# Gate weights in one transfer, and a new order of the work, in a kernel that fuses sparse attention with a mixture of experts

## The chip, the cores and the metric

The kernel runs on one core of a Trainium2 chip. The metric is the device time of one execution in microseconds (us); lower is better. Five engines work beside each other: TensorE (PE in the profile, PEld for its weight loads), VectorE (DVE), ScalarE (ACT), GpSimd (POOL) and SyncE (SP), whose queue here issues nearly all transfers.

## The reference, cut to what matters

Attention over 8 batches of 8 heads, 576 positions of 64 numbers; four heads look at the last 32 positions, four at every 32nd. Its output, 4608 tokens of 512 numbers, goes through a gate that picks one of 8 experts for each token; an expert keeps its 80 best tokens, and all other rows of the result are zero.

```python
scores = scale * np.matmul(q, k.transpose(0, 1, 3, 2))
scores = np.where(masks[None, :, :, :], scores, -1000000000.0)
attn = np.exp(scores - np.max(scores, axis=-1, keepdims=True))
attn = attn / (np.sum(attn, axis=-1, keepdims=True) + 1e-09)
x = np.matmul(attn, v) ...   # (4608, 512)
logits = x @ w_gate          # (512, 8)
expert_idx = np.argmax(logits, axis=1)
for e in range(E):
    ...                      # keep the `capacity` tokens with the largest gate_w
    h = np.maximum(x[tok_idx] @ w1[e], 0.0)
    out[tok_idx] = gate_w[tok_idx, None] * (h @ w2[e])
```

## The kernel before, in words

The kernel is a list of small operations with names, dependencies and an engine each (class `Plan`). A table of names (`ORDER`, lines 1048 to 1110) gives the order in which they are emitted; each engine, and SP's queue, runs its part of the table strictly in that order. A mark behind a name picks the engine (`/V` DVE, `/A` ACT, `/G` POOL) or the PSUM bank (a digit). A number behind a point is the batch.

*Attention, batch by batch.* SP loads the inputs (`lq`, `lk`, `sq`, `sk`, `lv`, `va`, `vb`, lines 340 to 357). For the local heads PE makes the scores (`sl0`, `sl1`, line 367), DVE the maxima and differences (`mx`, `sb`), ACT the exponentials (`ex`), DVE the sums (`sml`), POOL the division (`nl`, line 400), DVE a transpose (`trl`, line 402), POOL and ACT eight copies into place (`c4l`), PE the product with v (`pvl`, line 420), ACT and DVE the copies out of PSUM (`el`). The strided heads go the same way: `ss` (line 450), `mxs`, `sbs`, `exs` (ACT, line 466), `sms` (DVE, line 469), `ns`, `trs` (line 477), `c4s`, `pvs` (line 492), `es`. `va` and `vb` of a batch refill the buffer that `pvs` of the batch before has read.

*Gate and store.* PE multiplies the output by the gate weights (`gt0`, lines 513 and 516), and DVE turns the logits into gates (`ga`, `gb`, `gc`, `gd`). PE transposes the output back (`rl`, `rs`), ACT or DVE copies it into one of three buffers `xn` (`wl`, `ws`, line 202), and SP stores the buffer to a scratch tensor in HBM (`st0`, `st1`, line 613). Since there are three buffers, the copies of store number i wait until store i-3 has landed; the stores are numbered 2·batch + part, so `wl1.7` and `ws1.7` (number 15) wait for `st0.6` (number 12).

*Gate weights.* `wgt` holds the 512×8 gate weights twice, among zeros (`fwgt` fills them), in two layouts. Four transfers, `wgl0`, `wgl1`, `wgs0`, `wgs1` (lines 278 and 280), bring them from the plain matrix, each in 256 runs of 32 bytes; `gt0.0` waits for all four.

*Routing.* After the last batch, `r1` to `r16` find for every expert its tokens: `r3`, `r7`, `r9` on DVE, `r5` on POOL, `r6` on ACT (line 726), `r9` (lines 750 and 756) waiting for `r6`. Then eight gathers fetch the chosen tokens (`g0` to `g7`, line 810), once all stores have landed.

*Experts.* 64 weight chunks of 512 KiB come in by `w0` to `w63` (line 643); 56 of them are split into two half-width parts by ACT (`wh`, line 672) and DVE (`wo`, line 674). PE multiplies (`u`, line 855; `d`, lines 874 to 882). 18 transfers of 512 KiB, `z0` to `z17` (line 622), write zeros over the output before the results are scattered (`s`, line 901). The table puts `w` and `z` wherever SP is to issue them, so both also serve as fillers between the loads of attention.

Of the kernel before, what the change touches and what calls it, by code (L numbers as in the profile page):

```python
# [1048 lines left out]
lq.0 pid lqb.0 pib fkm0/V fkm1/G fwgt/A fkl1/A fkl0/V pm0 lk0.0 lk1.0 fkn0/A fpts1/V lkb1.0 lk0.1 pmc fks0/A lkb0.0  # L1049
lk1.1 pmn/V ps0 fkn1/A tk warm/4 sl0.0 lq.1 wgs0 fks1/G sk1.0 tk1/0 sq.0 mx0.0 sl1.0 sk0.0 sb0.0 lv.0 psc ex0.0 tk2  # L1050
rc1 mx1.0 lk1.2 sl0.1 lk0.2 sb1.0 lq.2 rc2 ex1.0 sl1.1 fpts0/A sml.0 fpsn/A lk0.3 sal.0/V srl.0 ss0.0 mx1.1 sk0.1
nl0.0 fptb0/A sk1.1 mx0.1 ss1.0 wgs1 nl1.0 fptb2/V ss2.0 sq.1 fptb1/G trl.0 ss3.0 sb0.1 c4l4.0/G c4l6.0/A sk1.2 sb1.1
c4l5.0/A lq.3 c4l1.0/G sl0.2 ex0.1 lk1.3 c4l3.0/G mxs.0 ex1.1 sk0.2 c4l7.0/G sbs.0 sl1.2 fzt/A c4l2.0/G sml.1 c4l0.0/G
exs.0 sal.1/V fvs1/A srl.1 sms.0 pvl0.0/1 nl0.1 fvs0/A sas.0/V srs.0 pvl1.0/2 mx0.2 ns1.0 nl1.1 el0.0/A vb.0 mx1.2
pvl2.0/0 va.0 ns0.0 ss0.1 trl.1 lv.1 lq.4 ss1.1 w0 sb0.2 c4l4.1/G c4l7.1/A ss2.1 cap trs.0 c4l1.1/A c4l5.1/G w1 ex0.2
sl0.3 c4l2.1/G wgl1 sb1.2 c4s3.0/G wgl0 ad1.0 ss3.1 c4s0.0/G w2 ex1.2 el1.0/V sq.2 c4s2.0/G ad2.0 c4s1.0/A sml.2
c4l6.1/G c4l3.1/A pvs0.0/1 c4l0.1/G el2.0/A sq.3 sal.2/V srl.2 mxs.1 pvl0.1/2 es0.0/A nl0.2 sk1.3 sbs.1 pvs2.0/0 lk0.4
nl1.2 el0.1/V exs.1 pvl1.1/1 es2.0/V wh0 pvs1.0/2 ad1.1 trl.2 pvl2.1/0 el1.1/A es1.0/A rl0.0/1 lv.2 ad2.1 c4l4.2/G
c4l0.2/A mx0.3 gt0.0/2 lk1.4 c4l5.2/A c4l3.2/G sb0.3 va.1 c4l6.2/A ss0.2 c4l7.2/G vb.1 sms.1 wl0.0/A sl1.3 sk0.3
sas.1/V el2.1/A srs.1 w3 wo0 ex0.3 w4 c4l2.2/A w5 rl0.1/1 xqs.0/V ns0.1 mx1.3 rs0.0/0 wl0.1/A ss1.2 sb1.3 ns1.1  # L1060
c4l1.2/A xql.0/G ss2.2 trs.1 ex1.3 pvl0.2/1 ws0.0/A sml.3 c4s2.1/G lt.0 st0.0 rl1.0/0 c4s0.1/G ss3.2 sal.3/V el0.2/A
c4s3.1/G srl.3 wl1.0/V pvl1.2/2 c4s1.1/A xql.1/G nl0.3 mxs.2 pvs0.1/1 ad1.2 pvl2.2/0 el1.2/A nl1.3 es0.1/V pvs1.1/2
ad2.2 sbs.2 pvs2.1/1 el2.2/A es1.1/A trl.3 rs1.0/0 vb.2 exs.2 sl0.4 lq.5 es2.1/A sms.2 w6 c4l1.3/G wh1 sas.2/V
c4l7.3/G srs.2 ws1.0/V wh2 c4l2.3/G sl1.4 mx0.4 c4l4.3/G c4l6.3/A sb0.4 c4l0.3/G gt0.1/2 ns1.2 ex0.4 lk1.6 mx1.4 ns0.2
c4l3.3/A lv.3 rl1.1/1 sb1.4 lk1.5 xql.2/G ss0.3 wo1 va.2 ex1.4 lk0.5 ss1.3 sk0.4 sml.4 rc3 gt1.0/0 z0 ss2.3 lt.1 z1
sal.4/V c4l5.3/A srl.4 z2 trs.2 ss3.3 nl1.4 sk1.4 pvl0.3/2 sq.4 ga.0 c4s0.2/G wl1.1/V pvl1.3/0 el0.3/A c4s1.2/G
c4s2.2/A rs0.1/1 xqs.1/G ad1.3 c4s3.2/G mxs.3 pvl2.3/2 ws0.1/A nl0.4 sbs.3 el1.3/A pvs1.2/1 ad2.3 pvs0.2/0 trl.4
es1.2/A exs.3 pvs2.2/1 el2.3/A c4l7.4/G sms.3 sl0.5 vb.3 es2.2/A c4l2.4/G sas.3/V es0.2/A st0.1 srs.3 c4l1.4/A lv.4
xqs.2/G sl1.5 mx0.5 ns0.3 wh3 st1.0 sb0.5 lq.6 c4l6.4/G lk0.6 rc4 ns1.3 va.3 gt0.2/2 trs.3 sk0.5 ss0.4 x0 mx1.5
c4s2.3/G rs1.2/1 sb1.5 rs1.1/0 ws1.2/A ss1.4 wo2 ex1.5 rs0.2/1 ex0.5 ss2.4 wo3 ws1.1/A ws0.2/A sml.5 c4s0.3/G gt1.1/0  # L1070
rl1.2/1 c4s1.3/G lt.2 ss3.4 c4l5.4/G sal.5/V wl1.2/A srl.5 rl0.2/2 c4l3.4/A c4l4.4/G mxs.4 sk0.6 sl0.6 c4s3.3/A nl0.5
z3 sbs.4 w7 ga.1 exs.4 sk1.5 c4l0.4/G pvs2.3/1 mx0.6 st1.1 wl0.2/A nl1.5 pvl0.4/0 sms.4 sq.5 es2.3/A pvs1.3/2 lk0.7
xql.3/A sas.4/V el0.4/V wh4 st0.2 pvl1.4/1 srs.4 es1.3/V pvs0.3/0 ns0.4 wh5 ad1.4 trl.5 pvl2.4/2 ns1.4 es0.3/A va.4
sl1.6 vb.4 trs.4 c4l7.5/G c4l3.5/A lv.5 c4l1.5/A sq.6 sb0.6 el1.4/A c4s1.4/G gt0.3/0 lk1.7 xqs.3/V c4l4.5/G ex0.6
sk1.6 ad2.4 mx1.6 gt1.2/1 c4l2.5/G lq.7 ss0.5 el2.4/V c4l0.5/G lt.3 sb1.6 rl0.3/2 c4s2.4/G rl2.3/0 ga.2 c4s0.4/G
wl0.3/A rl1.3/1 c4s3.4/G wl2.3/V xql.4/A rs2.3/2 ex1.6 c4l6.5/G ss1.5 ws2.3/V wl1.3/A pvs2.4/0 c4l5.5/A sml.6 pvs1.4/1
es2.4/A pvl0.5/2 wo4 es1.4/A pvs0.4/0 el0.5/A wo5 pvl1.5/1 wh6 vb.5 va.5 pvl2.5/2 sal.6/V srl.6 es0.4/V nl0.6 ss2.5
lv.6 xqs.4/V ad1.5 gb.2 el1.5/A ss3.5 nl1.6 rs0.3/0 ad2.5 sk0.7 mxs.5 el2.5/A sk1.7 gt0.4/1 sbs.5 ws0.3/A st1.2 trl.6
z4 exs.5 sl0.7 z5 z6 sms.5 c4l4.6/G c4l0.6/A gt1.3/2 st0.3 c4l5.6/A sas.5/V c4l2.6/G sl1.7 srs.5 sq.7 mx0.7 c4l6.6/G
z7 sb0.7 z8 c4l1.6/G ga.3 ss0.6 c4l7.6/G ex0.7 mx1.7 lt.4 ns0.5 ss1.6 c4l3.6/A sb1.7 ns1.5 ss2.6 ex1.7 trs.5 ss3.6  # L1080
sml.7 rl0.4/0 c4s3.5/A c4s1.5/G rl1.4/2 ge.2 c4s2.5/G wl0.4/A pvl0.6/1 sal.7/V c4s0.5/G srl.7 wl1.4/A mxs.6 rs1.3/0
nl0.7 el0.6/A sbs.6 gt1.4/2 ws1.3/A nl1.7 pvs2.5/1 ga.4 gc.2 pvs1.5/0 es2.5/A pvs0.5/2 exs.6 pvl1.6/1 es1.5/A sms.6
vb.6 es0.5/A st2.2 pvl2.6/0 sas.6/V srs.6 ad1.6 ns1.6 trl.7 gt0.5/2 el1.6/A ns0.6 lv.7 va.6 ss0.7 trs.6 c4l5.7/A st2.1
lt.5 st1.3 rs1.4/1 c4l7.7/A st2.3 gt1.5/2 c4s0.6/G c4s3.6/A w8 ss1.7 c4l3.7/G ga.5 c4l6.7/A w9 gd.2 ss2.7 c4l2.7/G
ws1.4/A gb.5 c4s2.6/G ss3.7 c4l0.7/G ad2.6 ge.5 el2.6/V rs0.4/2 c4l4.7/A c4s1.6/G mxs.7 rl0.5/1 ws0.4/A gr.2/0 sbs.7
st0.4 pvs1.6/2 gg.2 wl0.5/A st1.4 wo6 pvs2.6/0 exs.7 pvs0.6/1 es1.6/A xql.5/G sms.7 c4l1.7/G es2.6/A rs0.5/2 sas.7/V
va.7 es0.6/A srs.7 rl1.5/0 gc.5 ns1.7 vb.7 ws0.5/A ns0.7 gt0.6/1 st0.5 wl1.5/A trs.7 pvl0.7/2 lt.6 rs1.5/0 el0.7/A
c4s3.7/G pvl1.7/1 c4s1.7/A ws1.5/V c4s2.7/G c4s0.7/A gt1.6/2 st1.5 ad1.7 xqs.6/G el1.7/V pvl2.7/0 wh7 xql.6/G w10
# [62 lines left out]
```

## Time and profile before

| | |
|---|---|
| median of 3 runs | 263.83 us (262.11 to 265.59) |
| the profiled execution | 264.44 us |
| its span in the trace | 262.7 us |
| busy PE, DVE, ACT, POOL | 80%, 77%, 60%, 41% of the span |
| moved by DMA | 84.05 MB |

All times in the trace count from the start of the span; 1.7 us of the execution lie around it. In the timeline a row gives start, duration, engine, line, operation, out<-in, and in brackets the idle time of that engine just before and what ended it. An engine takes its instructions in order, so an idle time in brackets also delays everything behind it on that engine. A row of the stretches gives, for each, its length, the busy time of PE, PEld, DVE, ACT and POOL, the granted TensorE clock (1.00 is full), the busy share of the 16 DMA engines (1.03 is what they reach here) and GB/s.

### The profile page before, as it was taken

How to read it: one execution, taken by the hardware profiler on the slowest of the kernel's cores; microseconds unless marked ns; L12 is line 12 of the kernel's file. 1: busy time of each engine (PE TensorE's matmuls, PEld its weight loads, DVE VectorE, ACT ScalarE, POOL GpSimd, SP SyncE). 2: the span in 40 equal slices, each digit the busy share in tenths (PEclk: the TensorE clock that was granted, in tenths of full speed). 3: DMA queues.
4: the chain of work that ended last, by engine and by line, in shares of the span. 5: the costliest groups of instructions: out<-in, count | busy, mean ns of one | idle time of the engine just before them, and what ended most of it. 6: DMA issues, size and time to landing. Idle time of an engine off the chain costs nothing. (4 is left out here: it accounts for less than half of the span.)

```text
span 262.7 us, 9497 instructions
## 1 busy us (share of the span) xinstructions
PE 209.6 (80%) x4036; PEld 162.8 (62%) x4036; DVE 202.9 (77%) x358; ACT 157.8 (60%) x244; POOL 107.9 (41%) x156
## 2 busy tenths in 40 slices
...
GB/s 160 255 401 392 253 309 405 375 258 287 387 373 231 262 407 328 293 401 237 228 370 216 333 371 298 347 360 419 412 413 408 387 410 384 409 410 408 115 41 43
DMA packets 24783, 84.05 MB, mean 320 GB/s; under 512 B 4321, under 2 KB 4321, under 8 KB 24162
## 3 DMA queue, kind: packets, MB, share of 16 engines
...
q0 software_dynamic: 1024, 2.62, 2.8%
...
## 5 line engine op out<-in xcount | busy, mean ns | idle before, releaser
L204 POOL COPY ptb<-ptl 32x576 f32<-32x576 f32 (+1 forms) x39 | 26.4, 676 | 14.2 <-DVE ptl L402 9.2
L202 ACT COPY xn<-bk 128x512 f32<-128x512 f32 x28 | 16.1, 583 | 19.5 <-DMA xs<-xn 9.9
L420 PE MATMUL bk<-ptb,vl 128*64 128x160 f32 (+1 forms) x288 | 24.5, 307 | 3.3 <-POOL pl L400 1.7
L492 PE MATMUL bk<-pts,vs 128*64 128x72 f32 x512 | 22.5, 248 | 5.3 <-POOL pts L204 1.9
L492 PEld LDWEIGHTS bk<-pts,vs 128*64 128x64 f32 x512 | 21.3, 156 | 7.4 <-issue 3.3
L400 POOL TENSOR_TENSOR pl<-pl,sm 128x576 f32<-128x576 f32 x16 | 18.2, 1150 | 18.6 <-DVE sm L398 13.0
L420 PEld LDWEIGHTS bk<-ptb,vl 128*64 128x64 f32 x288 | 19.1, 140 | 4.9 <-issue 1.9
L450 PE MATMUL sstr<-ks,qs 128*18 128x36 f32 x1024 | 14.8, 199 | 8.2 <-issue 7.7
L202 ACT COPY ptb<-ptl 32x576 f32<-32x576 f32 (+1 forms) x25 | 16.6, 665 | 7.9 <-DVE ptl L402 7.6
L204 POOL COPY pts<-pts 32x576 f32<-32x576 f32 x24 | 17.0, 707 | 9.7 <-DVE pts L477 8.9
L901 POOL DMA_INDIRECT out<-xtl,pl x4 | 4.5, 1123 | 40.0 <-ACT xtl L896 22.3
L450 PEld LDWEIGHTS sstr<-ks,qs 128*18 128x18 f32 x1024 | 11.3, 99 | 12.7 <-issue 10.6
L474 POOL TENSOR_TENSOR psn<-ps,sm 128x64 f32<-128x64 f32 (+1 forms) x16 | 11.5, 738 | 16.7 <-DVE sm L472 6.5
L901 POOL DMA_INDIRECT out<-xts,pl x4 | 4.9, 1234 | 28.9 <-ACT xts L896 23.5
L386 ACT ACTIVATE pl<-pl 128x512 f32<-128x512 f32 (+1 forms) x16 | 10.7, 683 | 9.8 <-DVE pl L383 9.8
L674 DVE SCALAR_TENSOR_TENSOR slot<-slot,slot 128x1024 f16<-128x1024 f32 x13 | 16.0, 1254 | 0.7 <-ACT slot L672 0.6
L855 PEld LDWEIGHTS <-slot 128*128 128x128 f16 x288 | 14.4, 113 | 3.1 <-issue 3.1
L672 ACT ACTIVATE slot<-slot 128x1024 f16<-128x1024 f32 x13 | 13.5, 1054 | 1.1 <-DMA slot<-w 1.0
L202 ACT COPY xts<-bk 128x360 f32<-128x360 f32 (+1 forms) x19 | 9.4, 509 | 7.4 <-PE bk L492 5.6
L202 ACT COPY xtl<-bk 128x416 f32<-128x416 f32 (+2 forms) x17 | 8.2, 479 | 9.5 <-DVE xtl L434 4.3
L195 PE MATMUL sla<-identb 128*128 128x512 bf16 x33 | 10.7, 463 | 2.7 <-DVE identb L256 2.7
L592 PE MATMUL bk<-ident,xtl 128*128 128x128 f32 x64 | 12.4, 325 | 0.4 <-ACT xn L202 0.3
...
## 6 DMA issues: line engine op xcount, KB each, us to landing
...
```

Source lines behind the costliest of these rows:

```text
L195: nc.tensor.matmul(sla.rearrange("p (a b) -> p a b", b=P), identb, identb.unsqueeze(1).broadcast_to([P, 4, P]), start=True, stop=True)
L202: nc.scalar.copy(o, i)
L204: eng[e].tensor_copy(o, i)
L400: op("nl%d.%d" % (u, b), {"POOL": 1.17}, lambda e, u=u: nc.gpsimd.tensor_tensor(pl[:, u], pl[:, u], sm[:, 9 * u:9 * u + 9].unsqueeze(2).br ...
L420: nc.tensor.matmul(t[64 * u:64 * u + 64, n0:n0 + z], tvl[:, u, c], ptb[:, c, u, 0:z], start=(c == 3 * k), stop=(c == 3 * k + 2), tile_posi ...
L450: nc.tensor.matmul(so[32 * g:32 * g + 18, r8], tqs[h][:, g, rr], tks[h][:, :, g, rr], start=False, stop=r8 == 7, tile_position=(0, 32 * g))
L474: op("ns%d.%d" % (i, b), {"POOL": d}, lambda e, js=js, z0=z0, z1=z1, st_=st_: nc.gpsimd.tensor_tensor(psn[:, :, z0:z1:st_], ps[:, :, js], ...
L492: nc.tensor.matmul(t[64 * x:64 * x + 64, c:c + 72], tvs[:, r], pts4[:, 2 * (r % 16) + r // 16].rearrange("p h j -> p (h j)"), start=True, ...
L592: nc.tensor.transpose(t[:, x, c], xv[:, c, x, 128 * a:128 * a + 128] if a < 2 else xql[:, c, x].rearrange("p s b -> p (s b)"), ident)
L672: op("wh%d" % i, {"ACT": 1.05}, lambda e: nc.scalar.activation(hi(i), raw(i), AF.Copy, scale=SC), [st["w%d" % i]] + prev, filler=True)
L674: op("wo%d" % i, {"DVE": 1.24}, lambda e: nc.vector.scalar_tensor_tensor(lo(i), raw(i), SC, hi(i), op0=ALU.mult, op1=ALU.subtract), [st["w ...
L855: nc.tensor.matmul(o[:, f], w[:, n:n + P], x[:, a, c], start=(c == 0 and i == 0 and f == 0), stop=(c == 3 and i == 2), skip_group_check=True)
```

## The change

First, the host packs the gate weights into one array of 128 × 48 numbers, and one transfer `wg` brings it into `lt`, a buffer that is free until `lt.0`. Four small copies, together `wgc`, put the numbers into their places in `wgt`; the table gives them to POOL. `gt0.0` waits for `wgc` instead of four transfers.

Second, the whole table is replaced. Nearly every name stands in another place, and some copies and fills change engine.

```diff
-    for x in range(2):
-        dma("wgl%d" % x, 8192, lambda x=x: nc.sync.dma_start(
-            wgl[:, x::2, E * x:E * x + E], wg[0:256].rearrange("(c p) e -> p c e", p=P)), fills["wgt"])
-        dma("wgs%d" % x, 8192, lambda x=x: nc.sync.dma_start(
-            wgs[64 * x:64 * x + 64, :, E * x:E * x + E], wg[256:512].rearrange("(h d) e -> d h e", d=D)), fills["wgt"])
+    wgp = lt[:, 0:48].rearrange("p (c e) -> p c e", e=E)
+    dma("wg", 24576, lambda: nc.sync.dma_start(lt[:, 0:48], wg), [])
+
+    def wgc(e):
+        for x in range(2):
+            copy(e, wgl[:, x::2, E * x:E * x + E], wgp[:, 0:2])
+            copy(e, wgs[64 * x:64 * x + 64, :, E * x:E * x + E], wgp[64 * x:64 * x + 64, 2:6])
+
+    op("wgc", {"DVE": 0.45, "POOL": 0.8, "ACT": 1.0}, wgc, fills["wgt"] + [st["wg"]])
...
-           ([st[n] for n in ("wgl0", "wgl1", "wgs0", "wgs1")] if b == 0 else []), pairs=16, mode="m32", acquire=True)
+           ([st["wgc"]] if b == 0 else []), pairs=16, mode="m32", acquire=True)
...
-r6 z10 w17 w18 warm/9 r8 w19 r9 w20 z11 wo8 warm/2 r10 z12 z13 r11 wh10 r12 r13 g0 z14 r14 g1 warm/1 r15 z15 r16 wo9
+rs2.7/2 wl2.7/A r5 wl1.7/A rs1.7/0 ws2.7/A ws1.7/A st2.4 st1.7 x0 r6 st2.6 st2.7 st2.5 warm/9 r8 w17 wh7 r9 w18 w19
...
+    wgp = np.concatenate([w_gate[0:256].reshape(2, P, E).transpose(1, 0, 2),
+                          np.tile(w_gate[256:512].reshape(4, D, E).transpose(1, 0, 2), (2, 1, 1))], axis=1).reshape(P, 6 * E)
```

Two places of the new order matter below. The first is ACT around `exs.7`, the exponentials of the last batch. Before, the piece is (L466 is `exs.7`; the copies into `xn` are `wl` and `ws`, here of batches 4 and 5):

```order
L563 ACTIVATE gsm_126<-gsm_126 96x144
L202 COPY ptb_98<-ptl_102 32x18x32
L202 COPY xn_112<-bk_149 128x2x256
L202 COPY xn_111<-bk_148 128x2x256
L466 ACTIVATE ps_105<-ps_105 128x576
L202 COPY xts_108<-bk_149 128x72x5
```

Now it is (L470 is `exs.7`):

```order
L567 ACTIVATE gsm_126<-gsm_126 96x144
L202 COPY ptb_98<-ptl_102 32x18x32
L202 COPY xqs_115<-xts_109 128x128
L470 ACTIVATE ps_105<-ps_105 128x576
L202 COPY xts_108<-bk_149 128x72x6
L202 COPY xts_108<-bk_147 128x72x5
L202 COPY xts_108<-bk_148 128x72x5
L202 COPY xn_111<-bk_149 128x2x256
L202 COPY xn_111<-bk_147 128x2x256
```

The copy into `xn_111`, which waits for a store to land, stood just ahead of the exponentials and now stands four rows behind them.

The second place is SP's queue around `st0.6` (of the rows `xs<-xn` the one from `xn_110` in the last rows of each piece). Before, the transfers ahead of it are (`w` and `zt` are fillers of 512 KiB each):

```order
L643 DMA kl_91<-w 128x1024
L613 DMA xs<-xr_113 32x1024
L643 DMA kl_91<-w 128x1024
L643 DMA ql_89<-w 128x1024
L643 DMA ks_95<-w 128x1024 x2
L622 DMA out<-zt_117 128x1024
L643 DMA qs_93<-w 128x1024
L643 DMA kl_92<-w 128x1024
L613 DMA xs<-xn_110 128x1024
L613 DMA xs<-xn_111 128x1024
```

Now they are:

```order
L617 DMA xs<-xn_111 128x1024
L617 DMA xs<-xn_110 128x1024
L617 DMA xs<-xr_113 32x1024
L626 DMA out<-zt_117 128x1024 x3
L617 DMA xs<-xn_112 128x1024
L626 DMA out<-zt_117 128x1024 x3
L617 DMA xs<-xr_113 32x1024
L617 DMA xs<-xn_110 128x1024
L647 DMA kl_92<-w 128x1024
L617 DMA xs<-xn_112 128x1024
L617 DMA xs<-xn_111 128x1024
```

Eight fillers stood between the large stores and `st0.6`; now three stand directly ahead of it, behind one large store and three more fillers.

## Rows read from the trace of the kernel before

**Rows 1.** The page: its first line, and busy time of the engines

```profile
span 262.7 us, 9497 instructions
...
PE 209.6 (80%) x4036; PEld 162.8 (62%) x4036; DVE 202.9 (77%) x358; ACT 157.8 (60%) x244; POOL 107.9 (41%) x156
```

**Rows 2.** The waits of ACT: for whom, us in total, times, the longest

```profile
ACT xn L202 <- DMA xs<-xn: 9.9, 3, 4.1
...
ACT slot L672 <- DMA kl<-w: 7.9, 2, 5.9
```

**Rows 3.** Timeline of ACT, from 116 to 168 us

```profile
119.61 0.58 ACT L202 COPY xn<-bk 128x512 f32<-128x512 f32 x1 [2.39 <-DMA xs<-xn]
...
135.73 0.58 ACT L202 COPY xn<-bk 128x512 f32<-128x512 f32 x1 [3.41 <-DMA xs<-xn]
136.34 0.68 ACT L466 ACTIVATE ps<-ps 128x576 f32<-128x576 f32 x1
...
161.50 1.56 ACT L202 COPY xn<-bk 128x512 f32<-128x512 f32 x3 [4.09 <-DMA xs<-xn]
162.93 2.13 ACT L726 ACTIVATE pl<-pl,esel 128x80 bf16<-128x80 bf16 x8
```

**Rows 4.** Timeline of DVE, PE and POOL, 121 to 223 us

```profile
121.24 0.35 DVE L532 TENSOR_REDUCE lgs<-bk 96x48 f32<-96x192 f32 x1 [2.38 <-PE bk L527]
...
132.83 0.69 PE L492 MATMUL bk<-pts,vs 128*64 128x72 f32 x15 [0.77 <-DMA vs<-va]
...
137.06 0.75 DVE L469 TENSOR_REDUCE sm<-ps 128x32 f32<-128x576 f32 x1 [2.61 <-ACT ps L466]
...
165.10 0.55 DVE L750 SCALAR_TENSOR_TENSOR pl<-jc,pl 128x320 bf16<-128x320 f32 x1 [3.34 <-ACT pl L726]
...
168.34 1.21 POOL L810 DMA_INDIRECT xtl<-xs,pl  x1 [9.09 <-DVE pl L774]
...
222.52 1.22 DVE L674 SCALAR_TENSOR_TENSOR kl<-kl,slot 128x1024 f16<-128x1024 f32 x1 [5.05 <-ACT slot L672]
```

**Rows 5.** Timeline of SP's queue: stores, fillers and loads with their times of issue

```profile
108.36 3.14 SPq L622 DMA_DIRECT2D out<-zt  x3
111.59 1.19 SPq L613 DMA_DIRECT2D xs<-xn  x1
...
127.82 0.53 SPq L613 DMA_DIRECT2D xs<-xn  x1
...
144.28 0.42 SPq L643 DMA_DIRECT2D kl<-w  x1
...
149.53 0.43 SPq L643 DMA_DIRECT2D kl<-w  x1
153.48 0.83 SPq L613 DMA_DIRECT2D xs<-xn  x2
```

**Rows 6.** Six stretches: length, busy PE PEld DVE ACT POOL, clock, DMA share, GB/s

```profile
34.00:36.00 2.00, 1.58 (x30) 1.38 (x32) 1.90 (x5) 1.28 (x3) 1.86 (x3) 0.76 0.76 296
36.00:38.00 2.00, 1.81 (x20) 1.48 (x18) 1.01 (x2) 0.68 (x1) 1.67 (x2) 0.50 0.69 247
...
122.00:126.00 4.00, 4.00 (x78) 3.90 (x74) 2.69 (x9) 2.43 (x5) 0.81 (x2) 0.78 0.08 26
162.00:164.00 2.00, 0.43 (x2) 0.00 (x0) 0.00 (x0) 2.00 (x8) 0.00 (x0) 1.00 0.16 64
190.00:200.00 10.00, 10.00 (x235) 9.99 (x233) 8.94 (x11) 6.82 (x10) 1.36 (x1) 1.00 1.03 411
...
245.00:262.70 17.70, 11.36 (x228) 10.94 (x225) 10.63 (x13) 6.85 (x10) 3.70 (x3) 0.93 0.12 37
```

**Rows 7.** The gate weights' transfers (ns min/median/max to issue), and a small POOL copy

```profile
L280 SPq DMA_DIRECT2D wgt<-wg x2: 642/652/661, 7.4 to 18.4; - x2
L278 SPq DMA_DIRECT2D wgt<-wg x2: 472/723/974, 31.1 to 32.1; - x2
...
156.56 0.19 POOL L716 CAST pl<-pl 128x16 f32<-128x16 uint32 x1
```

More of the change, by code (lines that the diff above doesn't have):

```diff
@@ L1048 @@
 ORDER = """
[L1049 to L1088, printed above, removed]
```

81 lines of the change are left out of this document (60 added, 21 removed).

## The prediction

> **What bounds the kernel now.** I read the page first, then the waits of ACT, then the timelines of ACT, DVE and SP at the moments those waits name, and last the stretches by DMA share. On the page no engine is full: PE is busy 80% and DVE 77% of 262.7 us [rows 1]. The stretches say why. In 190 to 200 us the DMA engines run at share 1.03 and 411 GB/s [rows 6], and the weight stream looks like that until 245 us; before it, during attention, the same engines have holes (share 0.08 in 122 to 126 us, 0.16 in 162 to 164 us [rows 6]). So the end of the run is set by how many bytes are left when attention is over and by when that is. After the stream 17.7 us remain in which DMA does almost nothing (share 0.12) and PE and DVE finish [rows 6]; that tail stays.
>
> What makes attention late is one kind of wait that stands out among ACT's: copies into `xn` that wait for an older store to land, 9.9 us in three pieces [rows 2]. They end at 119.61, 135.73 and 161.50 us [rows 3]. Their stores (`st0.3`, `st1.3`, `st0.6`) were issued at 111.59, 127.82 and 153.48 us [rows 5]: 8.0, 7.9 and 8.0 us earlier. A store thus takes 8 us to land in this part of the run, and a copy that comes sooner stops ACT, with all that is queued behind it. DVE pays: 2.38 us of idle time before L532 at 121.24, 2.61 us before L469 at 137.06 (it waits for the exponentials `exs.7`, which ran at 136.34, right behind the stopped copy [rows 3]), and 3.34 us before L750 at 165.10 (it waits for `r6`, which ran at 162.93, behind the three copies) [rows 3, 4].
>
> **The change part by part.** The sum is made against the profiled execution's own 264.44 us; that is 0.61 us above the median of the runs, 263.83 us, and the forecast is brought to the median at the end.
>
> *The distance from a store to the copy that needs its buffer.* I count in the table how many DVE entries stand between a store and the first copy that must wait for it. Before: 11, 8 and 4 for the three pairs above. Now: 22, 24 and 5. All other pairs had 6 or more before and showed no wait. The first two waits should therefore go.
> - First wait (`st0.3`): DVE's 2.38 us. It is bounded by 0 (something else is late) and 3.2 us (with the wait that follows it a little later). Next late is POOL, which has the division and the copies of two batches queued there; I take 2.4.
> - Second wait (`st1.3`): the exponentials now stand ahead of the copies, so DVE's 2.61 us go. Next late is the v load of the last batch, whose product PE needs just after; PE already waited once for a load `va`, 0.77 us at 132.83 [rows 4]. Bounds 0 and 2.61; I take the middle, 1.3.
> - Third wait (`st0.6`): the distance is still 5 entries, so the copy comes as early as before. But ahead of the store there were eight fillers, issued from 144.28 to 149.53 us and a little after [rows 5]; one is 524,288 bytes, at 411 GB/s [rows 6] 1.28 us, so 10 us of traffic. Now three fillers stand directly ahead (3.8 us) and three more behind one store further up. Bounds 0 and 3.34; I take half, 1.7.
>
> *A pair that gets closer.* `st0.1` and the copy `wl1.2`: 5 DVE entries now, 7 to the nearest copy before. With 6 and 7 no wait showed, with 8 one of 3.41 us on ACT did [rows 3], because the queue was fuller there. Behind that copy on ACT stand two of the copies that PE's `pvl` of batch 4 waits for. Bounds 0 and 3.41; I take 1.0 lost.
>
> *Fillers.* Of the 82 fillers, 27 are issued before the last `st1.7` in the old table, 29 in the new one. Two fewer remain for the saturated stream: 2 × 1.28 = 2.6 us. The stream can use it, since DVE stood idle for 5.05 us at 217 to 222 us for a weight chunk [rows 4], and ACT 5.9 us for the same [rows 2]. Against it, one split fewer is done ahead of the expert phase (12 instead of 13): 1.22 us more on DVE later [rows 4]. Net 1.4 gained, bounds 0 and 2.6.
>
> *Gate weights.* Four transfers of 256 runs of 32 bytes become one of 128 runs of 192 bytes, and SP issues one row instead of four (0.65 to 0.72 us each [rows 7]). In 34 to 38 us, when two of the four and the `cap` load of 8-byte runs were in the queue, the DMA share was 0.76 and 0.69 [rows 6], a loss of (1.03-0.76)×2 + (1.03-0.69)×2 = 1.2 us for these together; the other two would cost as much at most, so at most 2.4 us. The new transfer has an eighth of the runs. Added are four POOL copies; the nearest small copy takes 0.19 us [rows 7], so 0.8 us on POOL, an engine at 41%, and ahead of the copies for `c4l.2`; uncovered they cost 0.8 us. Bounds: 2.4 gained, 0.8 lost. The early DMA time is worth little, since the same engines have holes later: I take 0.5 gained. Here a page speaks against the change: the Trainium skill, "DMA: Bandwidth & Descriptors", section "Specifications", says that below 512 bytes a run is not moved at line rate but by read-modify-write. By that mark alone 192 bytes are no better than 32, and this term would be nothing; the rows show a loss with short runs but not at which length it ends.
>
> *The sum.* -2.4 -1.3 -1.7 +1.0 -1.4 -0.5 = -6.3 us; 264.44 - 6.3 = 258.1, and 0.6 less on the median's scale: 257.5 us. All other moves I cost at nothing: up to `r1` the entries of both tables hold the same work, within 2 us on each engine (ACT has 4 us less), so what they do is only in which waits they make.
>
> **The rivals.**
>
> *More is gained.* If the new order also closes the holes of the DMA engines, 0.95 × 4 = 3.8 us in 122 to 126 us and 0.87 × 2 = 1.7 us in 162 to 164 us [rows 6] come on top, some 252 us. For it: weight fillers now stand ahead of the `va` and `vb` loads of the last two batches, where SP has to wait for PE and before had little in flight. Against it: the second hole is partly the third wait again.
>
> *No change.* The two waits go, but PE and DVE at 80% and 77% [rows 1] only find the next dependency late, as they do at a dozen smaller places; about a sixth of the sum is left, 263 us. For it: each idle time I count is the last of several things that come within 1 or 2 us. Against it: the two moved pairs do not get a little but twice to three times further apart.
>
> *Slower.* Three fillers now stand ahead of `va.6` and three more ahead of `lv.7` in the one queue. Each three cost 3.8 us of the load behind them. If neither is covered, 7.7 us of attention are lost, the three waits' gain does not show because the loads are later than they were, and only the fillers' 1.4 comes back: 264.44 + 7.7 - 1.4 - 0.6 = 270 us. It decides from the point where `va.6` lands after the last of the copies `c4s.6`. For it: PE has already waited for `va` there [rows 4]. Against it: SP waits for PE before it may issue these loads, and by then the fillers have had time to drain.
>
> **How the numbers follow.** Forecast, 257.5 us, with a range of its own of 254 to 261: 0.50. More gained, about 252: 0.20. No change, about 263: 0.16. Slower, about 270: 0.14. About 2% of the time, 5.3 us, is what a measurement of this kernel can tell from no change: faster means below 258.6, slower above 269.1. Of the forecast's case 0.28 lie below 258.6 and 0.22 above; the first rival adds 0.20 to faster, the second 0.16 to same, the third 0.13 to slower and 0.01 to same. So faster 0.48, same 0.39, slower 0.13. The range reaches into both rivals' sides: 251 to 267.
>
> **What would show each step right or wrong.** In the profile after, ACT's wait for `xs<-xn` should fall from 9.9 us to under 5, and what is left should stand before `r6`; L469 should not wait 2.6 us for the exponentials of the last batch; L750 should begin less than 3 us after the last instruction of `r7`; the first gather, now at 168.34 us [rows 4], should come near 163; the saturated stream should end near 239 us instead of 245. I am wrong if the gather comes no earlier, if the stream ends no earlier although it does, or if a new wait for `vs<-va` or `vl<-vl` of some microseconds stands before L492 or L420.

## The result, and the profile after

The changed kernel takes 251.22 us (median of 4 runs, 248.06 to 253.73), against 263.83 us before: a ratio of 0.9445, 95% interval 0.9316 to 0.9574. Run once more later, it took 250.65 us (248.03 to 253.98, 6 runs; ratio 0.9497, 0.9443 to 0.9552). Medians are of all runs; ratios are of those within 1.5% of the kernel's fastest. The forecast was 257.5 us: the direction is right, the size half of what came by the medians (6.3 of 12.6 us) and less than half by the ratio (14.6 us). The time lies below the forecast's own range, 254 to 261 us, and just inside the wide one, 251 to 267. The profiled execution took 248.06 us, with a span of 246.3 us.

The page after, its first line and the busy time of the engines, to be held against [rows 1]:

```profile
span 246.3 us, 9517 instructions
...
PE 202.8 (82%) x4037; PEld 157.7 (64%) x4037; DVE 206.9 (84%) x359; ACT 156.4 (63%) x243; POOL 108.9 (44%) x160
```

Each engine is busy for as long as before, within 7 us of 210; the span is 16.4 us shorter. So it is mostly idle time that went. The waits of ACT after (for whom, us in total, times, the longest):

```profile
ACT ptb L202 <- DVE ptl L406: 10.7, 3, 4.9
...
ACT slot L676 <- DMA kl<-w: 5.8, 1, 5.8
```

The 9.9 us of copies that waited for stores [rows 2] are gone altogether; the list has no such entry. The wait for a weight chunk in the expert phase is as long as before. The timeline of ACT, DVE, POOL and PE after, at the places that answer to [rows 3, 4]:

```profile
128.23 0.71 ACT L470 ACTIVATE ps<-ps 128x576 f32<-128x576 f32 x1
...
151.95 2.13 ACT L730 ACTIVATE pl<-pl,esel 128x80 bf16<-128x80 bf16 x8 [0.41 <-POOL pl L726]
...
128.97 0.76 DVE L473 TENSOR_REDUCE sm<-ps 128x32 f32<-128x576 f32 x1 [0.97 <-ACT ps L470]
...
154.37 0.54 DVE L754 SCALAR_TENSOR_TENSOR pl<-jc,pl 128x320 bf16<-128x320 f32 x1
...
157.40 1.22 POOL L814 DMA_INDIRECT xtl<-xs,pl  x1 [5.48 <-DVE pl L777]
...
89.75 0.46 PE L454 MATMUL sstr<-ks,qs 128*18 128x36 f32 x32
```

The exponentials of the last batch start 8 us earlier, `r6` 11 us earlier, the mask of `r9` (L754) without a wait, and the first gather at 157.40 instead of 168.34 us. The last row, the first strided scores of batch 5, has no counterpart in the rows of the prediction. Here it is in the kernel before, with SP's queue ahead of it (the first row, `x0`, stores a row of zeros in the scratch tensor):

```profile
77.14 0.48 SPq L283 DMA_DIRECT2D xs<-zt  x1
84.67 0.47 SPq L352 DMA_DIRECT2D ks<-ks  x1
...
88.05 0.43 SPq L350 DMA_DIRECT2D qs<-qs  x1
...
96.26 0.71 PE L450 MATMUL sstr<-ks,qs 128*18 128x36 f32 x32 [1.31 <-issue]
```

SP waited 7.0 us, from 77.6 to 84.67, for PE to finish with the buffer that the load `sk0.6` refills. Behind it stood `sq.5`, a load whose own buffer was free: it went out at 88.05, and the strided scores of batch 5 began at 96.26 us, 6.5 us later than now. That they waited for this load is not named there: the bracket says only "issue". In the changed kernel `sq.5` is issued at 69.64 us:

```profile
69.64 0.45 SPq L354 DMA_DIRECT2D qs<-qs  x1
...
109.80 1.41 SPq L359 DMA_DIRECT2D vl<-vl  x1
111.25 0.43 SPq L647 DMA_DIRECT2D slot<-w  x1
111.73 1.12 SPq L647 DMA_DIRECT2D kl<-w  x2
112.94 0.57 SPq L617 DMA_DIRECT2D xs<-xn  x1
115.39 0.53 SPq L360 DMA_DIRECT2D vs<-va  x1
```

The lower rows are a second place: three weight fillers go out just before SP comes to `va.6`, which has to wait for PE. Before, SP issued nothing from 116.5 to 124.6 us while it waited for PE, and the DMA engines' share fell to 0.08 from 122 to 126 us [rows 6].

What this does to the DMA engines stands in the stretches (columns as in [rows 6]; the share is the last but one). The kernel before:

```profile
0.00:80.00 80.00, 61.99 (x1490) 45.91 (x1491) 67.97 (x117) 48.56 (x75) 50.89 (x80) 0.96 0.90 323
...
80.00:100.00 20.00, 15.81 (x330) 12.61 (x329) 13.46 (x25) 12.18 (x22) 11.26 (x16) 0.91 0.83 299
100.00:120.00 20.00, 15.59 (x417) 12.24 (x417) 17.29 (x29) 10.55 (x19) 11.03 (x14) 1.00 0.92 345
120.00:140.00 20.00, 17.24 (x329) 14.25 (x333) 13.68 (x31) 11.95 (x23) 7.64 (x13) 0.77 0.73 258
140.00:150.00 10.00, 10.00 (x148) 7.06 (x149) 7.41 (x23) 6.08 (x12) 3.74 (x7) 0.96 0.79 274
150.00:160.00 10.00, 7.71 (x50) 5.50 (x51) 8.74 (x39) 5.24 (x9) 3.22 (x12) 1.00 1.02 386
160.00:170.00 10.00, 3.86 (x26) 1.91 (x25) 6.11 (x26) 4.62 (x12) 1.36 (x2) 0.74 0.85 303
```

The changed kernel, with the two holes of [rows 6] and the tail:

```profile
0.00:80.00 80.00, 64.42 (x1534) 47.92 (x1535) 68.96 (x113) 45.14 (x69) 51.47 (x86) 0.96 0.93 337
...
80.00:100.00 20.00, 17.71 (x433) 14.74 (x434) 18.63 (x34) 18.08 (x32) 10.39 (x11) 1.00 0.97 368
100.00:120.00 20.00, 16.91 (x418) 12.24 (x413) 17.71 (x35) 11.52 (x23) 14.34 (x21) 1.00 0.87 313
120.00:140.00 20.00, 16.05 (x298) 13.51 (x300) 14.84 (x38) 10.25 (x21) 10.04 (x16) 0.91 0.95 359
140.00:150.00 10.00, 7.74 (x77) 5.72 (x71) 9.43 (x32) 5.17 (x12) 1.72 (x7) 1.00 1.01 391
150.00:160.00 10.00, 6.49 (x40) 3.18 (x41) 9.47 (x37) 7.46 (x16) 3.76 (x8) 0.88 0.81 289
160.00:170.00 10.00, 7.08 (x66) 4.50 (x64) 6.54 (x10) 5.56 (x8) 4.83 (x4) 0.84 0.99 358
...
122.00:126.00 4.00, 4.00 (x96) 3.37 (x93) 2.87 (x4) 0.19 (x1) 0.21 (x1) 0.68 1.00 384
162.00:164.00 2.00, 0.94 (x5) 0.20 (x3) 0.66 (x1) 0.61 (x1) 1.70 (x2) 1.00 0.91 324
...
233.00:246.30 13.30, 6.67 (x120) 6.15 (x117) 6.98 (x9) 3.52 (x6) 2.75 (x2) 0.87 0.15 45
```

Take 1.03 minus the share, times the length, as idle time of the DMA engines. From 80 to 170 us it was 20 × (0.20 + 0.11 + 0.30) + 10 × (0.24 + 0.01 + 0.18) = 16.5 us and is 8.8; from 0 to 80 us it was 10.4 and is 8.0. The two falls, 7.7 and 2.4, are 10.1 of the 12 us by which the weight stream ends earlier (233 instead of 245 us). The tail behind the stream fell from 17.7 to 13.3 us, 4.4. The holes at 122 to 126 and 162 to 164 us are filled.

The clock column has changed too: from 120 to 140 us TensorE was granted 0.77 before and 0.91 after (a mix of its two levels, 0.50 for 1.2 and 1.00 for 2.4 GHz), over the whole profiled run 0.917 and 0.958. No run holds the clock fixed, so what part of the gain goes with it stays open. It is not what the largest single edit below gave (the fillers moved up as one train): that profile shows 0.907, and the time fell by 7.2 us.

### The profile page after: what moved, and what is told of

It is laid out like the page before. It is cut to its first block, busy times and chain, and to the rows that moved or that the text cites. A ratio compares the mean times of both kernels' runs of the same rounds, so it can differ in the third digit from the quotient of the medians.

```text
span 246.3 us, 9517 instructions
## 1 busy us (share of the span) xinstructions
PE 202.8 (82%) x4037; PEld 157.7 (64%) x4037; DVE 206.9 (84%) x359; ACT 156.4 (63%) x243; POOL 108.9 (44%) x160
## 5 line engine op out<-in xcount | busy, mean ns | idle before, releaser
L204 POOL COPY ptb<-ptl 32x576 f32<-32x576 f32 (+1 forms) x41 | 27.7, 676 | 11.8 <-PE bk L424 5.1
L202 ACT COPY ptb<-ptl 32x576 f32<-32x576 f32 (+1 forms) x23 | 15.3, 666 | 17.2 <-DVE ptl L406 10.7
L496 PE MATMUL bk<-pts,vs 128*64 128x72 f32 x512 | 20.1, 234 | 3.0 <-issue 1.2
L496 PEld LDWEIGHTS bk<-pts,vs 128*64 128x64 f32 x512 | 18.7, 143 | 4.5 <-issue 2.6
L204 POOL COPY pts<-pts 32x576 f32<-32x576 f32 x19 | 15.5, 818 | 10.3 <-DVE pts L481 7.8
L202 ACT COPY xn<-bk 128x512 f32<-128x512 f32 x25 | 13.9, 586 | 4.6 <-PE bk L596 3.3
L678 DVE SCALAR_TENSOR_TENSOR slot<-slot,slot 128x1024 f16<-128x1024 f32 x13 | 16.4, 1289 | 0.3 <-ACT slot L676 0.2
L859 PEld LDWEIGHTS <-slot 128*128 128x128 f16 x288 | 12.7, 104 | 2.6 <-issue 2.6
L478 POOL TENSOR_TENSOR psn<-ps,sm 128x64 f32<-128x64 f32 (+1 forms) x16 | 10.7, 687 | 7.1 <-ACT ptb L202 3.4
L371 PE MATMUL slb<-kl,ql 128*32 128x128 f32 x320 | 12.4, 301 | 1.5 <-issue 1.5
L195 PE MATMUL sla<-identb 128*128 128x512 bf16 x34 | 10.7, 457 | 2.7 <-DVE identb L256 2.7
L406 DVE STREAM_TRANSPOSE ptl<-pl 128x1152 f32<-128x1152 f32 x8 | 10.9, 1367 | 1.9 <-POOL pl L404 1.9
L371 PEld LDWEIGHTS slb<-kl,ql 128*32 128x32 f32 x320 | 9.5, 121 | 4.7 <-issue 4.4
```

Source lines behind the costliest of these rows:

```text
L195: nc.tensor.matmul(sla.rearrange("p (a b) -> p a b", b=P), identb, identb.unsqueeze(1).broadcast_to([P, 4, P]), start=True, stop=True)
L202: nc.scalar.copy(o, i)
L204: eng[e].tensor_copy(o, i)
L371: nc.tensor.matmul(o[32 * g:32 * g + 32, 128 * c - z:128 * c - z + 128], tql[h][:, hh, 32 * t:32 * t + 32], tkl[h][:, :, hh, 32 * t:32 * t ...
L406: op("trl.%d" % b, {"DVE": 1.37}, lambda e: nc.vector.transpose(ptl.rearrange("p u c s q -> p (u c s q)"), pl.rearrange("p u c k -> p (u c ...
L496: nc.tensor.matmul(t[64 * x:64 * x + 64, c:c + 72], tvs[:, r], pts4[:, 2 * (r % 16) + r // 16].rearrange("p h j -> p (h j)"), start=True, ...
```

## The experiments

18 kernels ran. The diffs show the table, mostly SP's part of it alone. Each ratio is to the kernel before, run on the same chip.

**The gate weights.** The changed kernel with the four old transfers:

```diff
-wg
+wgl0 wgl1 wgs0 wgs1
...
-wgc/G
```

> The changed kernel with the four old gate transfers in the place of the one, and without the four POOL copies; nothing else differs. Gate theory: the one transfer was worth what I gave it, 0.5 us, at most 2.4, so 251.7 to 253.6 us, and ACT and PE are late around gt0.0 at 40 us. All other theories: the DMA holes later swallow it, 250.5 to 252 us, no different from the changed kernel.

Measured: 250.65 us, ratio 0.9534 (0.9459 to 0.9609). That is the changed kernel's time; the gate edit is worth nothing that can be told. Its stretches behind the four loads, which SP issues from 30.9 to 33.6 us:

```profile
32.00:34.00 2.00, 1.51 (x58) 1.39 (x44) 1.88 (x5) 1.97 (x4) 1.62 (x3) 1.00 0.84 237
34.00:36.00 2.00, 1.88 (x41) 1.10 (x36) 1.97 (x3) 1.95 (x3) 0.31 (x1) 1.00 1.13 328
36.00:38.00 2.00, 0.01 (x2) 0.01 (x2) 2.00 (x4) 1.47 (x4) 1.51 (x1) 1.00 1.02 334
```

Here all four loads of short runs leave the share at 0.84 to 1.13; in the changed kernel, without them, it is 0.90, 0.99 and 1.00 in the same stretches. The 0.76 and 0.69 of [rows 6], which I had put down to them, were not their doing, or not theirs alone; the `cap` load, which stood beside them there, is at 79 us here.

**Queue or engines?** The two orders taken apart: first the changed kernel's engines with SP's queue of before, then the reverse.

```diff
-sk0.5 lk1.7 z3 lk0.7 st1.1 st0.2 sk0.6 va.4
+sk0.5 x0 sk0.6 z3 w7 sk1.5 st1.1 sq.5 lk0.7 st0.2 va.4
...
```

> The changed kernel's order on PE, DVE, ACT and POOL, but SP's queue in the order of the kernel before (the one gate transfer in the place of the four). Queue theory (the gain is that no load stands behind a blocked entry of SP's queue): about 260 us or more. Engine theory (the gain is in the order of the engines): about 253 us. Store theory (my prediction: stores too close to the copies that need their buffers): the engine distances stay long, the eight fillers ahead of st0.6 and the two fillers fewer come back, +1.7 and +1.4, about 254 us.

> The reverse: the order of the kernel before on the four engines (with the four gate copies put in on POOL), and SP's queue in the order of the changed kernel. Queue theory: 252 to 256 us. Engine theory: 262 us. Store theory: the copies into xn stand as close behind their stores as before, only the fillers ahead of st0.3 and st0.6 differ, about 260 us, with ACT's wait for stores at 5 us or more.

Measured: 283.39 us (1.071, 1.0604 to 1.0817) and 270.64 us (1.0258, 1.0172 to 1.0344). Both mixtures are slower than either kernel. That is "260 us or more" for the queue theory in the first; every other number missed. The DMA engines stood idle for about 44 and 36 us up to 170 us, against 27 in the kernel before (1.03 minus the share of that stretch, as above). A queue served strictly in order and the engines it waits for are one order; a half of each tells nothing of what the other half is worth. So I went on with small edits of the kernel before.

**The store waits, my theory.** All three waits taken away by the distances that I had counted, on the kernel before:

```diff
-st1.2 z4 z5 z6 st0.3 sq.7 z7 z8 vb.6 st2.2 lv.7 va.6 st2.1 st1.3 st2.3
+st1.2 st0.3 z4 z5 z6 sq.7 z7 z8 st1.3 vb.6 st2.2 lv.7 va.6 st2.1 st2.3
...
-wl0.5/A exs.7 es1.6/A es2.6/A
+exs.7 es1.6/A es2.6/A wl0.5/A
...
-w10 st2.0 w11 w12 w13 w14 z9 w15 w16 st0.6 st1.6
+w10 st2.0 st0.6 st1.6 w11 w12 w13 w14 z9 w15 w16
```

> The kernel before with only its three store waits taken away: three fillers put behind st0.3, wl0.5 behind es2.6, st1.3 ahead of vb.6, seven fillers put behind st1.6. Store theory: ACT's wait for stores falls from 9.9 us to under 3 and the time by 2.4 + 1.3 + 1.7 = 5.4 us, to 258.4 us. Queue theory and engine theory: the waits go but little else, 261 to 264 us.

Measured: 263.47 us, ratio 0.9965 (0.9916 to 1.0014): no change. The waits did go (0.3 us are left), the last strided transpose (`trs.7`, L477) ran 4.4 us earlier (136.04 instead of 140.39 us), and then this stood in POOL's timeline, with these stretches before it:

```profile
170.47 1.21 POOL L810 DMA_INDIRECT xtl<-xs,pl  x1 [15.50 <-DMA out<-zt]
...
120.00:140.00 20.00, 16.54 (x357) 12.81 (x358) 16.28 (x35) 13.37 (x25) 10.59 (x18) 1.00 0.89 328
140.00:150.00 10.00, 8.70 (x125) 6.76 (x124) 8.41 (x35) 5.92 (x13) 1.35 (x2) 1.00 0.36 120
```

The seven fillers that I put behind `st1.6` left a new hole at 140 to 150 us (share 0.36), and then stood ahead of the last six stores. `r11` had the gathers' row numbers ready at 159.8 us (159.62 + 0.16); the last 10.7 us of the gather's 15.5 are its wait for those stores. The profile names a filler (`out<-zt`) instead, but the gather depends on none. The wait had moved, and the idle time of the DMA engines with it: their share from 0 to 170 us is 0.87, as in the kernel before.

The same without the third piece, so that no filler moves past the last stores:

> The kernel before with its first two store waits taken away and no filler put further back past the last stores: three fillers behind st0.3, wl0.5 behind es2.6, st1.3 ahead of vb.6. Store theory: trs of the last batch 3.7 us earlier and all of it at the end, 260 us. Hole theory (the time is the bytes moved, plus what the DMA engines stand idle until the stream ends, plus the tail): the time falls by what the idle time of 100 to 170 us falls by and no more; if that stays at 12 to 13 us, no change, 263 to 264 us.

Measured: 259.67 us, ratio 0.9856 (0.9779 to 0.9933). `trs.7` ran at 134.72 us, and the median fell by 3.6 us, the sum of my first two terms (2.4 + 1.3 = 3.7); by the interval it is 1.8 to 5.8 us. The share from 0 to 170 us rose from 0.87 to 0.90, some 5 us less idle time, so this run does not part the store theory from the hole theory.

**Fillers moved up as one train.** On the kernel before, all fillers from `z3` on three places further up:

```diff
-sk0.5 x0 sk0.6 z3 w7 sk1.5
+sk0.5 z3 w7 z4 x0 sk0.6 sk1.5
...
-st1.2 z4 z5 z6 st0.3 sq.7 z7 z8 vb.6 st2.2 lv.7 va.6 st2.1 st1.3 st2.3 w8 w9
+st1.2 z5 z6 st0.3 sq.7 z7 z8 w8 w9 w10 vb.6 st2.2 lv.7 va.6 st2.1 st1.3 st2.3 w11 w12
 st0.4 st1.4 va.7 vb.7 st0.5 st1.5
-w10 st2.0 w11 w12 w13 w14 z9 w15 w16 st0.6
+w13 st2.0 w14 z9 w15 w16 st0.6
```

> The kernel before with the fillers moved up in SP's queue by three: three of them ahead of x0 and sk0.6, three more ahead of vb.6, the rest closing up, so that four instead of seven stand ahead of st0.6. The number issued before the last store stays 27. Hole theory: the holes at 82 to 86 and 122 to 126 us are filled, 5 to 6 us, and the third store wait shrinks by 3 us: 257 to 260 us. Store theory: only the third wait counts, 262 us. Rival (fillers delay the loads behind them): 264 to 268 us.

Measured: 256.07 us, ratio 0.971 (0.9655 to 0.9765), 7.2 us off the median: the largest single part. First a row of the kernel before, the hole that had no row yet; then the edited kernel at the two holes, and its tail:

```profile
82.00:86.00 4.00, 3.77 (x56) 2.68 (x55) 1.29 (x2) 2.32 (x4) 2.79 (x3) 0.60 0.26 68
...
82.00:86.00 4.00, 3.88 (x56) 2.96 (x55) 1.07 (x2) 2.11 (x4) 2.79 (x3) 0.50 1.00 405
...
122.00:126.00 4.00, 4.00 (x84) 2.92 (x81) 2.92 (x4) 2.32 (x5) 1.54 (x3) 1.00 0.82 257
...
236.00:254.60 18.60, 12.18 (x251) 11.76 (x248) 11.20 (x13) 7.25 (x10) 3.71 (x3) 0.92 0.16 53
```

Both are filled, the wait ahead of `r6` is gone, and the first gather is at 160.89 us. Then each third of this edit alone: `z3 w7 z4` ahead of `x0`; `w8 w9 w10` ahead of `vb.6`; `w10 w11 w12` from ahead of `st0.6` to behind `w9`.

```diff
-sk0.5 x0 sk0.6 z3 w7 sk1.5
+sk0.5 z3 w7 z4 x0 sk0.6 sk1.5
```

> One third of the fillers-ahead run: only z3, w7 and z4 moved ahead of x0 and sk0.6, to fill the hole of the DMA engines at 82 to 86 us. Hole theory: 3 x 1.28 us less idle time in 80 to 100 us, 260 to 261 us. Theory that holes in the middle only move: 263 us, with the idle time coming back in 100 to 140 us.

```diff
-z7 z8 vb.6 st2.2 lv.7 va.6 st2.1 st1.3 st2.3 w8 w9 st0.4
+z7 z8 w8 w9 w10 vb.6 st2.2 lv.7 va.6 st2.1 st1.3 st2.3 st0.4
```

> Another third: only w8, w9 and w10 moved ahead of vb.6, to fill the hole at 122 to 126 us. Hole theory: 260 to 261 us. Theory that the hole only moves (the stretch behind, 128 to 140 us, loses these fillers): 263 us.

```diff
-w8 w9 st0.4 st1.4 va.7 vb.7 st0.5 st1.5 w10 st2.0 w11 w12 w13
+w8 w9 w10 w11 w12 st0.4 st1.4 va.7 vb.7 st0.5 st1.5 st2.0 w13
```

> The last third: only w10, w11 and w12 moved from ahead of st0.6 to behind w9, so that the store that r6 waits for has five instead of seven or eight fillers ahead of it. Store theory (my third term, 1.7 us, at most 3.3): 260.5 to 262 us, with the first gather 2 to 3 us earlier than 168.34. Hole theory: the idle time at 160 to 170 us falls by 1 to 2 us, 261.5 to 262.5 us.

Measured: 261.41 us (256.04 to 262.8, no interval; before in the same runs 263.77); 263.13 us, ratio 1.0016 (0.9968 to 1.0065); 264.66 us, ratio 0.9968 (0.9907 to 1.003). The last two are no change. The first is 2.4 us by the medians, but one of its four runs, 256.04 us, is as fast as the whole edit, and the others lie at 260.7 to 262.8: what it is worth stays open. The whole gave 7.2. The second third, in one stretch and in ACT's waits:

```profile
122.00:126.00 4.00, 4.00 (x80) 3.64 (x80) 2.88 (x8) 2.56 (x5) 1.20 (x2) 0.87 0.71 281
...
ACT xn L202 <- DMA xs<-xn: 15.8, 5, 4.9
```

The hole is filled (0.08 before, 0.71 now), but seven fillers still stand ahead of the last stores, and ACT waits longer for stores than before, 15.8 us instead of 9.9 [rows 2]. The last third took the wait ahead of `r6` away, but `r6` ran no earlier (163.13 us, before 162.93); ACT waited 16.9 us for other stores instead. And the whole edit does not win by shorter waits for stores; ACT still has 9.3 us of them. What it changes is the idle time of the DMA engines, here from 0 to 170 us in the kernel before and with the whole edit, then ACT's waits with it:

```profile
0.00:170.00 170.00, 132.21 (x2784) 99.48 (x2785) 134.66 (x285) 99.18 (x168) 89.14 (x142) 0.92 0.87 315
0.00:170.00 170.00, 137.31 (x2799) 102.54 (x2805) 139.99 (x289) 103.02 (x173) 95.71 (x146) 0.91 0.91 332
...
ACT xn L202 <- DMA xs<-xn: 9.3, 5, 4.4
```

A share of 0.91 instead of 0.87 is some 7 us less idle time. The thirds, in profiled runs of 262.8, 263.9 and 264.7 us, have 0.88, 0.87 and 0.86: in the first the hole at 80 to 100 us is filled (0.83 before, 0.99), and comes back at 100 to 170 us (0.85 before, 0.82).

**Loads ahead of a blocked entry.** On the kernel before:

```diff
-sk0.5 x0 sk0.6 z3 w7 sk1.5 st1.1 sq.5 lk0.7
+sk0.5 sk1.5 sq.5 x0 sk0.6 z3 w7 st1.1 lk0.7
```

> The kernel before with two loads, sk1.5 and sq.5, moved ahead of x0 and sk0.6, the entry of SP's queue that waits 7 us for PE at 77 to 84 us; nothing else. Queue theory (loads stood behind a blocked entry): the loads go out near 78 us, the idle time of the DMA engines in 80 to 100 us falls from 4.0 to under 2, trs of batch 5 comes 4 us or more earlier than 114.45, and the time is 259 to 261 us. My prediction, which costed all such moves at nothing: 262.5 to 265 us.

Measured: 261.77 us, ratio 0.9942 (0.9884 to 1.0), with `trs.5` 1.9 us earlier, at 112.52; not clear by itself. The mirrored edit, on the changed kernel:

```diff
-lv.4 cap lq.7 sk1.5 sk0.5
+lv.4 cap lq.7 sk0.5
...
-lq.6 sq.5 st0.1
+lq.6 st0.1
...
-st0.2 sk0.6 va.4
+st0.2 sk0.6 sk1.5 sq.5 va.4
```

> The changed kernel with sk1.5 and sq.5 put behind sk0.6 in SP's queue, as they stood before; nothing else. Queue theory: the first strided scores of batch 5, at 89.75 us in the changed kernel and at 96.26 before, go back to 95 us or later, trs of batch 5 from 106.23 to 110 us or later, and the time rises by 1.5 (what the mirrored edit gave) to 4 us, 252.5 to 255 us. Theory that such moves cost nothing: 250 to 252 us.

Measured: 254.59 us, ratio 0.9635 (0.9584 to 0.9687), above the interval of the changed kernel run beside it (0.9443 to 0.9552): 3.9 us lost by the medians, with two names of the table. The load goes out at 88.81 us and PE stops for it:

```profile
88.81 0.40 SPq L354 DMA_DIRECT2D qs<-qs  x1
...
97.53 0.68 PE L454 MATMUL sstr<-ks,qs 128*18 128x36 f32 x32 [6.21 <-DMA qs<-qs]
```

`trs.5` falls back to 114.73 us, where the kernel before had it (114.45).

**The expert phase.** The kernel before up to `r11`, from there on the changed kernel's order:

```diff
-r11 wh10 r12 r13 g0 z14 r14 g1 warm/1 r15 z15 r16 wo9
+r11 w21 r12 r13 warm/1 g0 r14 z14 g2 r15 warm/15 z15 g1 w22 z16 wo9
...
```

> The kernel before up to r11 (the token numbers for the gathers); from there on every engine and SP's queue in the order of the changed kernel. Tail theory (of the profiled 16.4 us, 4.4 are the stretch after the weight stream, 18.7 us before and 14.3 after, and it is the order of the expert phase that makes it): 4 us less than the kernel before, about 259.5 us, with the stream ending as before at 244 us. Store theory and hole theory (all that counts is ahead of the gathers): no change, 262 to 265 us.

Measured: 261.97 us, ratio 0.9945 (0.9871 to 1.002). Its tail in the profile is short, 14.4 us behind 244 us, where the kernel before had 18.7:

```profile
244.00:258.40 14.40, 7.27 (x128) 6.75 (x127) 7.62 (x9) 4.12 (x6) 3.11 (x3) 0.83 0.15 44
```

**All four together**, on the kernel before, still with its old gate transfers and its old order of attention:

> The kernel before with the four edits of the runs before together: the first two store waits taken away, sk1.5 and sq.5 ahead of sk0.6, the fillers moved up by three, and the expert phase in the order of the changed kernel; the old gate transfers and the old order of attention stay. If these four are the change (their medians fell by 3.6, 1.5, 7.2 and 1.3 us, 13.6 in all): 249 to 253 us, the time of the changed kernel. If they take the same idle time away twice: 254 to 257 us, and the rest of the gain lies in the thousand other places of the order.

Measured: 252.04 us, ratio 0.9608 (0.9493 to 0.9722). That is the changed kernel's time within the uncertainty (251.22 and 250.65). Copies wait for stores for 0.4 us in all, and POOL's timeline and the two stretches read like the changed kernel's:

```profile
158.27 1.21 POOL L810 DMA_INDIRECT xtl<-xs,pl  x1 [5.42 <-DVE pl L772]
...
82.00:86.00 4.00, 4.00 (x108) 3.26 (x99) 2.96 (x7) 3.11 (x6) 3.08 (x4) 1.00 1.02 390
...
122.00:126.00 4.00, 2.63 (x135) 2.09 (x136) 2.27 (x6) 3.56 (x6) 2.46 (x5) 1.00 0.99 396
```

The same without the new expert order:

> The kernel with all four edits but the expert phase in the order of the kernel before. Tail theory: the stream ends where it did (234 us) and 18 instead of 15 us follow it, 255.5 to 256.5 us. If the expert order is worth only the 1.3 us that its own run showed: 253 to 254 us.

Measured: 254.55 us, ratio 0.9622 (0.9572 to 0.9671). By the medians the expert order is worth 2.5 us here and 1.3 us in its own run; by the ratios, 0.9608 against 0.9622 with overlapping intervals, nothing that can be told. The tail in the profiles is 18.8 us without it and 15.9 with it. Its size stays open, between nothing and 4 us.

**The changed kernel, its train moved.** Back by three:

```diff
-lv.6 w9 w10 w11 st1.3 va.6 vb.6 w12 w13 w14 st0.4 lv.7 w15 vb.7 va.7 st0.5 st1.4 st2.3 z6 z7 z8 st1.5
+lv.6 st1.3 va.6 vb.6 w9 w10 w11 st0.4 lv.7 w12 vb.7 va.7 st0.5 st1.4 st2.3 w13 w14 w15 st1.5 z6 z7 z8
```

> The changed kernel with its own fillers moved back in SP's queue by three (none ahead of va.6 and vb.6, three instead of six behind them and ahead of lv.7, six instead of three ahead of st0.6); the number ahead of the last store stays 29, the engines keep their order. Train theory (what counts is that the fillers as a whole stand far enough ahead to flow while SP waits at a blocked entry, so that the stores behind them find a short queue): 256 to 259 us, with idle time of the DMA engines at 110 to 135 us and a wait of ACT for xs<-xn ahead of r6. Theory that the engines' order makes the gain: 251 to 253 us.

Measured: 255.0 us, ratio 0.9557 (0.9484 to 0.9629). By the medians that is 4.3 us more than the changed kernel run again, by the ratios 0.6% or 1.6 us, with overlapping intervals: not clear, and less than expected. ACT's waits name no store, against what I expected, but ACT stands idle just ahead of the copies before `r6`:

```profile
151.43 0.58 ACT L202 COPY xr<-bk 128x512 f32<-128x512 f32 x1 [5.73 <-issue]
```

The profile names no releaser. The copy refills `xr`, whose last store SP had issued at 143.02 us, behind six fillers, 8.4 us earlier; in the changed kernel run again ACT waits 2.0 us there, for PE, and `r6` runs at 151.00 instead of 154.12 us. That fits the train theory and is not shown. The first gather starts 2.5 us after its row numbers are ready, in the changed kernel run again 2.3: it is not the gather that pays.

Further up by three, and the kernel with four edits by two:

```diff
-va.5 st2.2 st2.0
+va.5 z6 z7 st2.2 st2.0
...
-st0.4 lv.7 w15 vb.7 va.7 st0.5 st1.4 st2.3 z6 z7 z8 st1.5
+st0.4 z8 lv.7 w15 vb.7 va.7 st0.5 st1.4 st2.3 st1.5
```

> The changed kernel with its fillers moved up by three more: two ahead of st2.2, where SP waits from 102 to 108 us, one ahead of lv.7, where it waits from 119 to 127 us, none left ahead of st1.5. Train theory: the idle time at 107 to 113 and 127 to 129 us is filled, 2 to 3 us, 248 to 250 us, faster than both kernels. Rival (two fillers delay sk1.7 and lv.6 of the batch behind): 252 to 254 us.

```diff
-lq.7 vb.5 va.5
+lq.7 z5 z6 vb.5 va.5
...
-st0.3 z5 z6 sq.7 z7 z8 w8 w9 w10 st1.3
+st0.3 sq.7 z7 z8 w8 w9 w10 w11 w12 st1.3
...
-st2.3 w11 w12 st0.4 st1.4 va.7 vb.7 st0.5 st1.5 w13 st2.0 w14 z9 w15 w16 st0.6
+st2.3 w13 w14 st0.4 st1.4 va.7 vb.7 st0.5 st1.5 z9 st2.0 w15 w16 st0.6
```

> The kernel with all four edits and its fillers moved up by two more: two ahead of vb.5, where the DMA engines stood idle from 101 to 104 us, the rest closing up, two ahead of st0.6. Train theory: 2 to 3 us less than the 252.0 of the four edits, 249 to 250.5 us. Rival (vb.5 and va.5 come later and PE waits for them): 253 to 255 us.

And the reference for the runs on the changed kernel:

> The changed kernel itself once more, so that the runs on it have a nearer reference than its first four times: 250 to 252 us. If the further train is a gain of its own (249.35 us), this stays at 250.5 us or above; if it comes out near 249 us, the two are the same.

Measured: 249.35 us, ratio 0.9438 (0.9383 to 0.9494); 252.01 us, ratio 0.9467 (0.9388 to 0.9547); and 250.65 us for the changed kernel again. The first is 1.3 us below it with overlapping intervals, the second has the median of the four edits (252.04) and a lower ratio (0.9467 against 0.9608), again with overlapping intervals: no version was shown to beat the changed kernel.

## Why the prediction was right in sign and too small

*What bounds the kernel: right.* The end is set by when the DMA engines have moved the bytes. The traces bear it out: idle time up to 170 us and the end of the weight stream fall together, about 27 and 245 us before, 22 and 239 with the two waits gone, 20 and 237 with the train moved, 19 and 236 with all four edits, 17 and 233 after. What I did not do was draw the consequence: the sum should have been made of their idle time, not of the engines' waits.

*First and second store wait, 2.4 + 1.3: right within what can be told.* Alone they gave 3.6 us, by the interval 1.8 to 5.8; that the sum fits to 0.1 us is luck, since `trs.7` came 5.7 us earlier. That they pay only while the fillers keep the queue full, as the run without gain showed, I had not seen.

*Third wait, 1.7: the wait went, but it is not what pays.* I counted the fillers directly ahead of `st0.6`. Moving three of them from there to ahead of `st0.4` does take the wait away, yet `r6` ran no earlier and the time stayed; moving seven behind it gave the wait to the gather. It pays when the whole train stands earlier.

*The closer pair, +1.0: did not come.* No copy waits for a store in the changed kernel.

*Two fillers more ahead of the last store, 1.4:* not tried alone. The wait for the chunk on which I had built it is still there, 5.8 us after and 5.9 before [rows 2].

*Gate weights, 0.5: nothing to be seen.* The four POOL copies cost 0.19 to 0.21 us each, as assumed. The loss that I read from [rows 6] does not come back with the four old loads (share 0.84 to 1.13). The rule of the Trainium skill ("DMA: Bandwidth & Descriptors", "Specifications"), by which this term would be nothing, gave the better number. No run here shows whether that is for the rule's reason.

*"All other moves I cost at nothing": this is the step that failed.* I had argued that both tables hold the same work up to `r1`, so that moves matter only by the waits they make, and then looked for those waits on ACT alone. SP's queue waits too: 7.0 us at `sk0.6` before. What stands behind a blocked entry is late: two loads there are worth 3.9 us in the changed kernel and about 1.5, not clear by itself, in the kernel before. And while SP is blocked only what was issued ahead of it flows. Moving the train up by three took off 7.2 us, of which my sum had the third wait, 1.7. With the two waits, the loads and the expert order this reaches the changed kernel's time. I had named the holes as a rival (some 252 us, chance 0.20); its number was the right one, and its doubt, that the second hole is partly the third wait again, was right as well. That the number came out is in part luck: its two holes are 5.2 of the 10.1 us of idle time that went, and the tail, which it left alone, gave 4.4.

*"That tail stays": wrong in the profiles,* 17.7 us to 13.3. Two pairs of profiles put it down to the order of the expert phase (18.7 and 14.4 us, 18.8 and 15.9); its size in the medians stays open.

*The slower rival:* fillers ahead of `va.6` and `lv.7` cost nothing; no wait for either stands in PE's waits after, where the kernel before had 0.77 us for `va` [rows 4].
